# Attention and gated FFN on one core: forty normalisations shared with ScalarE, the weights' check moved behind the last scores

## The chip, the cores and the metric

The kernel runs on one core of a Trainium2 chip. A core has five engines that run side by side: TensorE (PE; its weight loads are listed as PEld), VectorE (DVE), ScalarE (ACT), GpSimd (POOL) and SyncE (SP), which here only issues transfers. Each engine takes its instructions in the order in which they were written or scheduled, and waits on semaphores for the others. The metric is the device time of one execution in microseconds (us), the median over runs.

## The reference

Attention over 4 batches, 8 heads, 768 tokens and 64 dimensions. Each query sees the 96 keys up to itself and the first 8 keys, with a bias that falls with the distance by a slope of the head. The heads' outputs are put side by side (512 columns) and go through a feed-forward part with float64 weights.

```python
scores = scale * np.matmul(q, k.transpose(0, 1, 3, 2)) + bias
scores = np.where(keep, scores, -1000000000.0)
scores = scores - np.max(scores, axis=-1, keepdims=True)
a = np.exp(scores)
a = a / (np.sum(a, axis=-1, keepdims=True) + 1e-09)
x = np.matmul(a, v)                        # to (4, 768, 512)
h = np.maximum(x @ w_in, 0.0)              # 512 -> 1024
conv_out[t] = sum(conv_w[k] * h[t + k - 1] for k in range(3))
out = h * (1.0 / (1.0 + np.exp(-conv_out))) @ w_out   # 1024 -> 512
```

## The kernel before

**Steps.** The attention is cut into 32 jobs, each for one batch, one half of the tokens (384) and one pair of heads, and each job into 3 steps of 128 queries: 96 steps. A step has the scores of both heads (PE, L351 in the first 9 jobs, L361 later), `maxima` (DVE, L378: bias and extremum in one pass over 232 columns, then a read of the sum register), `exps` (ACT, L390, one for each head, whose row sums go to `mm[:, 2:4]`), `normalise`, `transposes` (PE L410 and L411, evicted by ACT at L414, L415 or L417), and once in three steps `values` (PE L433) and `mixed` (ACT L445, DVE L446). `normalise` adds 1e-9 to both sums (DVE, L398), takes the reciprocals (DVE, L399) and scales the two heads' probabilities in place, both on GpSimd (POOL, L402). The probabilities lie in three buffers (`pbuf`) that the steps take in turn. Transposes follow two steps behind the scores (`LAG_T`), values four.

**The feed-forward part** runs beside the attention in 8 units of 384 tokens, from a queue that `fill` works off by costs: mm1 (PE L464, early pieces L485), relu (ACT L474, into `hbuf`), the convolution (POOL L510, DVE L511 and L512), the gate (ACT L530 and, for a test on saturation, L541), the split into two parts (DVE L563, ACT L565, DVE L566), mm2 (PE L575) and the eviction (ACT L589). The matmuls' results of both go to three banks of `ps_m`. The last unit follows behind the last step.

**The weights** come as 64-bit words, in 16 pieces of 128 x 512 (512 KB each). DVE makes float32 of them by bit operations (L290, L292, L294), POOL casts the high part (L299) and DVE forms the low part (L305). `piece_check` tests that the words' exponents are in the range which these bit operations need: ACT squares the high words and sums them up (L312), then a relu with a large scale, summed up too (L315). `check_weights` at the end turns the sums into a flag, by which a general path would be taken; it isn't with these inputs. The chores are kept in lists (`chores`), one for each engine, and a budget per step (`work`) says how much of each is issued.

**The order.** In steps 0 to 10 (`HAND`) every engine follows the order of the code: scores, values, transposes, `normalise(s - 1)`, `maxima(s)`, `exps(s)`, mixed, then chores. From step 11 on a list scheduler orders the instructions of each engine by an estimated timeline and the priorities of the code.

Of the kernel before, what the change touches and what calls it, by code (L numbers as in the profile page):

```python
# [9 lines left out]
F32 = mybir.dt.float32  # L10
F32R = mybir.dt.float32r
BF16 = mybir.dt.bfloat16
I32 = mybir.dt.int32
U32 = mybir.dt.uint32
AF = mybir.ActivationFunctionType
# [5 lines left out]
P = 128  # L21
# [13 lines left out]
LAG_T, LAG_V = 2, 4  # L35
NPB = 3
HAND = 11
NATIVE = 9
# [24 lines left out]
def fast_path(tc, io):  # L63
# [152 lines left out]
    odd, red, flag = rest[:, 0:3], rest[:, 3:7], rest[:, 7:8].bitcast(I32)  # L216
    bad, ones, ebias, gbias, least = (rest[:, k : k + 1] for k in range(8, 13))
    G.memset(gbias, -0.96)
    G.memset(least, 1.5)

# [85 lines left out]

    def piece_check(i, half, n):
        k = 2 * i + half
        if n == 0:
            squares[k] = p1.tile([P, HW], F32, tag="ob", name=f"square{k}")  # L310
            x = wraw[i, half][:, :, 1].bitcast(F32)
            A.activation(squares[k], x, AF.Square, accum_out=chk[:, NCHK + k : NCHK + k + 1])  # L312
        else:
            y = squares[k]
            A.activation(  # L315
                y, y, AF.Relu, bias=least, scale=-(2.0**30), accum_out=chk[:, k : k + 1]
            )

    squares = {}

    def check_weights():
        small, large = chk[:, :NCHK], chk[:, NCHK:]
        V.tensor_scalar(small, small, 0.0, None, ALU.is_gt)
        V.tensor_scalar(large, large, 2.0**30, None, ALU.is_le)
        V.tensor_scalar(large, large, -1.0, 1.0, ALU.mult, ALU.add)
        V.tensor_reduce(red[:, 0:1], chk, axis=mybir.AxisListType.X, op=ALU.max)
        V.tensor_tensor(bad, bad, red[:, 0:1], ALU.add)
# [57 lines left out]
    def exps(s):  # L385
        m, i = steps[s]
        sp, c0, n, mm = st_s[s]
        pb = pbuf[s % NPB]
        for j in range(2):
            last_exp[s] = A.activation(  # L390
                pb[:, j, c0 : c0 + n], sp[j][:, c0 : c0 + n], AF.Exp,
                bias=mm[:, j : j + 1], scale=-1.0, accum_out=mm[:, 2 + j : 3 + j],
            )
        st_s[s] = (pb, c0, n, mm)

    def normalise(s):
        pb, c0, n, mm = st_s[s]
        V.tensor_scalar(mm[:, 4:6], mm[:, 2:4], 1.0e-9, None, ALU.add)  # L398
        V.reciprocal(mm[:, 6:8], mm[:, 4:6])  # L399
        for j in range(2):  # L400
            x = pb[:, j, c0 : c0 + n]
            G.tensor_scalar(x, x, mm[:, 6 + j : 7 + j], 1.0, ALU.mult, ALU.mult)  # L402

# [240 lines left out]

    queue, cur = [], {}
    last_exp, last_mm, last_ev = {}, {}, {}

    def fill(k):
        with contextlib.ExitStack() as es:
# [7 lines left out]
            while queue and (k > 0 or queue[0][0] == 0):  # L657
                cost, fn, a = queue.pop(0)
                fn(*a)
                k -= cost  # L660

    chores = {"dve": [], "pool": [], "act": []}

# [11 lines left out]
    def piece_bits(i, half, n):  # L675
        weight_bits(i, half, n)
        if n == 0:
            for k in range(2):
                chores["act"].append((cur["s"], 0.9, piece_check, (i, half, k)))
        if n == 2:  # L680
# [32 lines left out]
    for s in range(len(steps) + LAG_V + 1):  # L713
        cur["s"] = s
        m, i = steps[s] if s < len(steps) else (len(jobs), -1)
        if s < HAND:
# [3 lines left out]
            if s >= LAG_T:  # L720
                transposes(s - LAG_T)
            if s:
                normalise(s - 1)
            maxima(s)
            exps(s)
            if ends(s - LAG_V - 1):
# [15 lines left out]
            work("pool", 1.3)  # L742
            work("act", 0.8)
        else:
# [30 lines left out]
            if s < len(steps):  # L775
                budget = DECODE_LATER[min((s - HAND) // 3, len(DECODE_LATER) - 1)]
                with tc.issue_after(last_ttr[s].ins):
                    work("dve", budget)
                    work("pool", 1.2)
                    work("act", 0.8)  # L780
        if s == 0:
# [14 lines left out]
        if s >= NB and i == 0:  # L796
            load_v(m)
    fill(10**9)

    def last_tiles():  # L800
# [173 lines left out]
```

## Time and profile before

| | before |
|---|---|
| runs, median (from, to) | 479.29 us (476.66 to 855.67), 3 runs |
| the profiled execution | 476.23 us |
| its span | 474.4 us |
| busy PE / DVE / ACT / POOL | 453.7 / 355.9 / 293.4 / 250.1 us |
| granted clock of PE, mean | 0.96 |

A row of windows gives, for one stretch of the span, the busy time and the number of instructions of each engine, the granted clock of PE as a share of full speed, and the share of the DMA engines. A row of lines gives one line's instructions on one engine: their number, the busy time of all in us and the mean of one in ns, and the engine's idle time ahead of them with what ended it. A chain of waits is followed back from the last instruction: at each step to what released it.

### The profile page before, as it was taken

How to read it: one execution, taken by the hardware profiler on the slowest of the kernel's cores; microseconds unless marked ns; L12 is line 12 of the kernel's file. 1: busy time of each engine (PE TensorE's matmuls, PEld its weight loads, DVE VectorE, ACT ScalarE, POOL GpSimd, SP SyncE). 2: the span in 40 equal slices, each digit the busy share in tenths (PEclk: the TensorE clock that was granted, in tenths of full speed). 3: DMA queues.
4: the chain of work that ended last, by engine and by line, in shares of the span. 5: the costliest groups of instructions: out<-in, count | busy, mean ns of one | idle time of the engine just before them, and what ended most of it. 6: DMA issues, size and time to landing. Idle time of an engine off the chain costs nothing.

```text
span 474.4 us, 8982 instructions
## 1 busy us (share of the span) xinstructions
PE 453.7 (96%) x3013; PEld 388.4 (82%) x3013; DVE 355.9 (75%) x936; ACT 293.4 (62%) x806; POOL 250.1 (53%) x351
## 2 busy tenths in 40 slices
PE   7989999969988999999999999999999999999994
PEld 6756688759866899888988998889988998899883
DVE  5889879995998999875798997866798877225600
ACT  2658767875947767754677677654677496335410
POOL 4544364873795597354766766555666754012000
PEclk8877599989998999999999999999999999999999
DMA  7856944223323433243324413433324201100111
GB/s 192 225 158 181 307 121 128 85 86 109 114 100 110 136 123 102 88 123 131 108 80 154 149 55 102 148 125 132 113 75 145 81 1 56 46 24 0 44 46 51
DMA packets 19062, 51.63 MB, mean 109 GB/s; under 512 B 2624, under 2 KB 2880, under 8 KB 19008
## 3 DMA queue, kind: packets, MB, share of 16 engines
q1 hardware_dynamic: 15552, 44.82, 31.0%
q10 hardware_dynamic: 3456, 6.16, 3.4%
q8 instruction: 26, 0.43, 0.4%
q14 instruction: 28, 0.23, 0.2%
HBM read 44.68 MB, written 6.29 MB: 107 GB/s over the span
## 4 chain that ended last, share of the span: by engine, by line
PE 77%; DVE 15%; ACT 2%; issue 2%; POOL 1%; DMA 1%; SPq 0%; POOLq 0%; DVEq 0%; ACTq 0%
PE o L575 26%; PE h L464 25%; PE pv L433 9%; PE s L361 5%; PE s L351 4%; PE t L410 4%; PE t L411 3%; DVE s L378 2%; DVE gl L566 1%; DVE c L511 1%; ACT pbuf L390 1%; DVE c L512 1%; DVE c L563 1%; DMA rq<-in_qk 1%; POOL pbuf L402 1%
## 5 line engine op out<-in xcount | busy, mean ns | idle before, releaser
L402 POOL TENSOR_SCALAR pbuf<-pbuf,mm 128x232 f32<-128x232 f32 (+1 forms) x192 | 137.6, 728 | 88.6 <-DVE mm L399 60.7
L390 ACT ACTIVATE pbuf<-s,mm 128x232 f32<-128x232 f32 (+1 forms) x192 | 83.5, 440 | 62.7 <-DVE mm L378 38.5
L378 DVE CUSTOM_DVE_ANT_0 s<-s,tab 128x232 f32<-128x232 f32 (+1 forms) x192 | 73.6, 385 | 24.6 <-PE s L361 16.9
L575 PE MATMUL o<-woh,gh 128*128 128x512 f32 x192 | 77.4, 403 | 0.0
L575 PE MATMUL o<-wol,gh 128*128 128x512 f32 x192 | 76.4, 398 | 0.0
L575 PE MATMUL o<-woh,gl 128*128 128x512 f32 x192 | 75.7, 395 | 0.0
L510 POOL TENSOR_SCALAR c<-hbuf,cw 128x382 f32<-128x382 f32 (+1 forms) x64 | 47.8, 751 | 51.5 <-ACT hbuf L474 51.5
L433 PE MATMUL pv<-pt,v 104*64 104x128 f32 (+2 forms) x768 | 57.4, 292 | 3.0 <-ACT pt L417 2.7
L464 PE MATMUL h<-xh,wih 128*128 128x384 f32 x252 | 59.8, 350 | 0.0
L464 PE MATMUL h<-xl,wih 128*128 128x384 f32 x252 | 59.2, 343 | 0.0
L464 PE MATMUL h<-xh,wil 128*128 128x384 f32 x252 | 57.9, 343 | 0.0
L433 PEld LDWEIGHTS pv<-pt,v 104*64 104x64 f32 (+2 forms) x768 | 43.2, 142 | 17.4 <-issue 10.0
L511 DVE SCALAR_TENSOR_TENSOR c<-hbuf,cw,c 128x382 f32<-128x382 f32 (+1 forms) x64 | 43.8, 691 | 16.6 <-POOL c L510 16.3
L417 ACT ACTIVATE pt<-t 128x512 f32<-128x512 f32 x80 | 48.0, 603 | 12.1 <-PE t L411 11.9
L410 PE MATMUL t<-ident,pbuf 128*128 128x128 f32 (+1 forms) x192 | 51.3, 286 | 3.9 <-POOL pbuf L402 3.3
L411 PE MATMUL t<-ident,pbuf 128*128 128x128 f32 x192 | 50.4, 281 | 0.0
L474 ACT ACTIVATE hbuf<-h 128x384 f32<-128x384 f32 x64 | 31.8, 498 | 25.8 <-PE h L464 25.7
L512 DVE SCALAR_TENSOR_TENSOR c<-hbuf,cw,c 128x382 f32<-128x382 f32 (+1 forms) x64 | 45.3, 711 | 0.5
L464 PEld LDWEIGHTS h<-xl,wih 128*128 128x128 f32 x252 | 44.2, 188 | 1.8 <-issue 1.8
L464 PEld LDWEIGHTS h<-xh,wih 128*128 128x128 f32 x252 | 44.0, 192 | 1.9 <-issue 1.6
L464 PEld LDWEIGHTS h<-xh,wil 128*128 128x128 f32 x252 | 44.0, 188 | 0.6 <-issue 0.5
L575 PEld LDWEIGHTS o<-woh,gl 128*128 128x128 f32 x192 | 36.3, 189 | 7.5 <-issue 0.2
(107 smaller groups left out, 858.5 us busy)
## 6 DMA issues: line engine op xcount, KB each, us to landing
v<-in_vv SPq DMA_DIRECT2D x32, 384.0 KB, 3.3
rq<-in_qk SPq DMA_DIRECT2D x23, 384.0 KB, 3.2
wr<-in_w SPq DMA_DIRECT2D x16, 512.0 KB, 5.0
rk<-in_qk SPq DMA_DIRECT2D x12, 504.0 KB, 3.5
out<-ob ACTq DMA_DIRECT2D x23, 256.0 KB, 2.0
rk<-in_qk SPq DMA_DIRECT2D x11, 408.0 KB, 3.7
rq<-in_qk SPq DMA_DIRECT2D x9, 192.0 KB, 6.0
rk<-in_qk SPq DMA_DIRECT2D x5, 204.0 KB, 5.9
```

Of the source, the lines that this page charges most:

```text
L378: last_ttr[s] = V.tensor_tensor_reduce(out=sp[j][:, c0 : c0 + n], in0=sp[j][:, c0 : c0 + n], in1=tb, scale=-0.125, scalar=3.0e38, op0=ALU. ...
L390: last_exp[s] = A.activation(pb[:, j, c0 : c0 + n], sp[j][:, c0 : c0 + n], AF.Exp, bias=mm[:, j : j + 1], scale=-1.0, accum_out=mm[:, 2 + ...
L402: G.tensor_scalar(x, x, mm[:, 6 + j : 7 + j], 1.0, ALU.mult, ALU.mult)
L410: T.transpose(pt[:ka, j, 0, :], pb[:, j, c0:P], ident)
L411: T.transpose(pt[:, j, 1, :], pb[:, j, P:256], ident)
L417: last_ev[s] = A.activation(sb, pt, AF.Copy)
L433: T.matmul(pv[m][64 * j : 64 * j + 64, i * P : (i + 1) * P], vt[m][:n, i, c, 64 * j : 64 * j + 64], sb[:n, j, c, :], start=c == 0, stop=c ...
L464: T.matmul(ps[:, :TB], w_[:, k, fs], x_, start=part == 0 and k == 0, stop=part == 2 and k == NK - 1,)
L510: G.tensor_scalar(c, *tap(1), 1.0, ALU.mult, ALU.mult)
L511: V.scalar_tensor_tensor(c, *tap(0), c, ALU.mult, ALU.add)
L512: V.scalar_tensor_tensor(c, *tap(2), c, ALU.mult, ALU.add)
L575: T.matmul(ps, g_[:, f], w_[:, f], start=f == 0 and part == 0, stop=f == NF - 1 and part == 2,)
```

## The change

In the first 40 steps (`SHARED`) the addition of 1e-9 goes from DVE to ACT, right behind the exps; DVE keeps the reciprocals; the second head is scaled by ACT, the first by POOL as before. In the hand-written steps `normalise(s - 1)` now comes behind `maxima(s)` and `exps(s)`. `piece_check` and its two ACT instructions for each piece are gone from the beginning. In their place the words are loaded again behind the last scores, 16 transfers of 512 KB with three buffers in turn, and each piece is tested by one reduction on DVE (the largest negated square) and one square with a sum on ACT, one piece for every three units of cost that `fill` issues.

```diff
-    bad, ones, ebias, gbias, least = (rest[:, k : k + 1] for k in range(8, 13))
+    bad, ones, ebias, gbias, eps = (rest[:, k : k + 1] for k in range(8, 13))
-    G.memset(least, 1.5)
+    G.memset(eps, 1.0e-9)
...
-    def piece_check(i, half, n):
-        k = 2 * i + half
-        if n == 0:
-            squares[k] = p1.tile([P, HW], F32, tag="ob", name=f"square{k}")
-            x = wraw[i, half][:, :, 1].bitcast(F32)
-            A.activation(squares[k], x, AF.Square, accum_out=chk[:, NCHK + k : NCHK + k + 1])
-        else:
-            y = squares[k]
-            A.activation(
-                y, y, AF.Relu, bias=least, scale=-(2.0**30), accum_out=chk[:, k : k + 1]
-            )
...
+    def check_load():
+        k = len(words)
+        X, tag = ((p2, "kk"), (p2, "kk"), (p1, "rk"))[k % 3]
+        t = X.tile([P, HW, 2], I32, tag=tag, name=f"check{k}")
+        nc.sync.dma_start(t, weight_words(*divmod(k, 2)))
+        words.append(t[:, :, 1].bitcast(F32))
+
+    def check_piece(k):
+        x = words[k]
+        junk = p2.tile([P, HW], F32, tag="qh", name=f"junk{k}")
+        j2 = p2.tile([P, HW], F32, tag="ql", name=f"junkb{k}")
+        V.tensor_tensor_reduce(
+            out=junk, in0=x, in1=x, scale=-1.0, scalar=-3.0e38,
+            op0=ALU.mult, op1=ALU.max, accum_out=chk[:, k : k + 1],
+        )
+        A.activation(j2, x, AF.Square, accum_out=chk[:, NCHK + k : NCHK + k + 1])
+        if len(words) < NCHK:
+            check_load()
...
+        if s < SHARED:
+            A.activation(mm[:, 4:6], mm[:, 2:4], AF.Identity, bias=eps)
...
-        V.tensor_scalar(mm[:, 4:6], mm[:, 2:4], 1.0e-9, None, ALU.add)
+        if s >= SHARED:
+            V.tensor_scalar(mm[:, 4:6], mm[:, 2:4], 1.0e-9, None, ALU.add)
         V.reciprocal(mm[:, 6:8], mm[:, 4:6])
         for j in range(2):
-            x = pb[:, j, c0 : c0 + n]
-            G.tensor_scalar(x, x, mm[:, 6 + j : 7 + j], 1.0, ALU.mult, ALU.mult)
+            x, inv = pb[:, j, c0 : c0 + n], mm[:, 6 + j : 7 + j]
+            if j and s < SHARED:
+                A.activation(x, x, AF.Copy, scale=inv)
+            else:
+                G.tensor_scalar(x, x, inv, 1.0, ALU.mult, ALU.mult)
...
+    def check_some(cost):
+        pace[0] += cost
+        while pace[1] < NCHK and pace[0] >= CHECK_EVERY * (pace[1] + 1):
+            check_piece(pace[1])
+            pace[1] += 1
...
                 fn(*a)
                 k -= cost
+                if words:
+                    check_some(cost)
...
+            maxima(s)
+            exps(s)
             if s:
                 normalise(s - 1)
-            maxima(s)
-            exps(s)
...
+        if s == len(steps):
+            for k in range(3):
+                check_load()
```

On DVE, in a hand-written step, behind the three bit operations of a weight piece (`w`, from the words `wr`), the order before was this (`mm` are a step's 128x8 small numbers, `s` its scores; the second L378 of a pair reads the sum register):

```order
L292 SCALAR_TENSOR_TENSOR w_0_381<-wr_0_249,w_0_381 128x512
L398 TENSOR_SCALAR mm_355<-mm_355 128x2
L399 RECIPROCAL mm_355<-mm_355 128x2
L378 ISA s_386,mm_401<-s_386,tab 128x232
L378 ISA mm_401 128x1
```

The same place now, where the lines are L294 for L292, L387 for L378 and L411 for L399:

```order
L294 SCALAR_TENSOR_TENSOR w_0_377<-wr_0_248,w_0_377 128x512
L387 ISA s_381,mm_392<-s_381,tab 128x232
L387 ISA mm_392 128x1
L387 ISA s_381,mm_392<-s_381,tab 128x232
L387 ISA mm_392 128x1
L411 RECIPROCAL mm_347<-mm_347 128x2
```

The addition is gone, and the reciprocal of the step before stands behind both maxima of this step.

On ACT, at the end of the first unit of the feed-forward part, the relu into `hbuf` of its last block h_7 was followed by a test, the eviction of a job's values (`xh`) and the exps of a step:

```order
L474 ACTIVATE hbuf<-h_7_1288 128x384
L541 ACTIVATE sat_2_1372,misc<-c_882,misc 128x2x382
L445 ACTIVATE xh_1359<-pv_1308 128x384
L474 ACTIVATE hbuf<-h_0_1377 128x384
L530 ACTIVATE c_882<-c_882 128x2x382
L390 ACTIVATE pbuf_193,mm_1354<-s_1349,mm_1354 128x232
```

Now (L489 is the relu, L405 the addition, L415 the second head's scaling, L432 an eviction of transposes):

```order
L489 ACTIVATE hbuf<-h_7_1251 128x384
L556 ACTIVATE sat_2_1332,misc<-c_859,misc 128x2x382
L405 ACTIVATE mm_1234<-mm_1234,misc 128x2
L405 ACTIVATE mm_1261<-mm_1261,misc 128x2
L460 ACTIVATE xh_1320<-pv_1270 128x384
L415 ACTIVATE pbuf_194<-pbuf_194,mm_1234 128x232
L432 ACTIVATE pt_1291<-t_1286 128x512
L415 ACTIVATE pbuf_192<-pbuf_192,mm_1261 128x136
```

The additions of two steps have come behind the relu of h_7, and the scalings of the same two steps behind `xh`.

On ACT in the last unit the relus of blocks 0 to 3 stood next to each other, with one gate and its test between:

```order
L474 ACTIVATE hbuf<-h_0_5097 128x384
L474 ACTIVATE hbuf<-h_1_5111 128x384
L474 ACTIVATE hbuf<-h_2_5129 128x384
L530 ACTIVATE c_5120<-c_5120 128x772
L541 ACTIVATE sat_0_5164,misc<-c_5120,misc 128x772
L474 ACTIVATE hbuf<-h_3_5147 128x384
```

Now squares of the check (L326) stand among them:

```order
L326 ACTIVATE junkb_5165,misc<-check_5100 128x512
L489 ACTIVATE hbuf<-h_0_5091 128x384
L489 ACTIVATE hbuf<-h_1_5111 128x384
L326 ACTIVATE junkb_5190,misc<-check_5120 128x512
L489 ACTIVATE hbuf<-h_2_5135 128x384
L326 ACTIVATE junkb_5214,misc<-check_5144 128x512
L545 ACTIVATE c_5126<-c_5126 128x772
L326 ACTIVATE junkb_5239,misc<-check_5168 128x512
L556 ACTIVATE sat_0_5182,misc<-c_5126,misc 128x772
L489 ACTIVATE hbuf<-h_3_5159 128x384
```

Ten of the 16 squares stand ahead of the relu of block 0, six behind that of block 1.

## Rows read from the trace of the kernel before

**Rows 1.** Windows: start:end, length; busy of PE, PEld, DVE, ACT, POOL; PEclk; DMA; GB/s.

```profile
0.00:46.00 46.00, 39.83 (x287) 30.34 (x289) 35.39 (x122) 25.82 (x87) 22.22 (x61) 0.81 0.71 194
46.00:94.00 48.00, 48.00 (x292) 37.03 (x292) 42.84 (x127) 36.22 (x111) 26.97 (x41) 0.86 0.51 155
94.00:164.00 70.00, 62.19 (x427) 53.56 (x427) 61.45 (x152) 50.34 (x139) 46.41 (x55) 0.95 0.34 110
164.00:396.00 232.00, 231.59 (x1633) 205.56 (x1632) 189.41 (x498) 154.72 (x426) 145.15 (x183) 1.00 0.33 107
396.00:474.40 78.40, 72.05 (x381) 61.90 (x379) 26.78 (x41) 26.26 (x48) 9.36 (x12) 0.99 0.10 35
```

**Rows 2.** Chain of waits, first 62 us: shares by line, then start, length, what.

```profile
by line: PE s L351 15.8%; DMA rq<-in_qk 7.8%; DVE s L378 7.6%; PE pv L433 7.3%; DVE w L292 6.2%; DVE w L294 6.1%; DVE wil L305 5.0%; ACT pbuf L390 4.6%; DVE w L290 3.8%; DVE mm L398 3.6%; PE h L485 3.5%; PE t L410 3.4%; POOL pbuf L402 3.4%;
...
2.25 4.85 DMA rq<-in_qk
```

**Rows 3.** Windows of 4 us, columns as in rows 1.

```profile
100.00:104.00 4.00, 1.03 (x9) 0.73 (x7) 3.90 (x13) 2.19 (x6) 2.29 (x4) 0.99 0.00 0
104.00:108.00 4.00, 4.00 (x32) 3.39 (x31) 3.37 (x10) 2.44 (x9) 3.26 (x5) 0.58 0.29 100
```

**Rows 4.** End of the whole chain of waits: start, length, what.

```profile
418.58 16.66 PE h L464 x96
435.25 32.70 PE o L575 x144
```

**Rows 5.** Windows of line L398 alone: DVE busy, PEclk, DMA share, GB/s.

```profile
0.00:46.00 46.00, 3.31 (x11) 0.81 0.71 194
46.00:94.00 48.00, 3.81 (x13) 0.86 0.51 155
94.00:164.00 70.00, 4.55 (x16) 0.95 0.34 110
```

**Rows 6.** Lines, the addition: xcount | busy us, mean ns | idle before, releaser.

```profile
L398 DVE TENSOR_SCALAR mm<-mm 128x2 f32<-128x2 f32 x96 | 24.4, 254 | 22.7 <-ACT pbuf L390 22.4
```

**Rows 7.** Waits up to 46 us: us in total, times, longest.

```profile
DVE mm L398 <- ACT pbuf L390: 2.6, 4, 0.9
```

**Rows 8.** Windows of line L402 alone: POOL busy, PEclk, DMA share, GB/s.

```profile
46.00:94.00 48.00, 13.83 (x24) 0.86 0.51 155
94.00:164.00 70.00, 26.35 (x33) 0.95 0.34 110
```

**Rows 9.** Timeline of DVE: start, length, line, operation.

```profile
99.72 0.96 DVE L511 SCALAR_TENSOR_TENSOR c<-hbuf,cw,c 128x382 f32<-128x382 f32 x1
...
101.76 0.60 DVE L511 SCALAR_TENSOR_TENSOR c<-hbuf,cw,c 128x382 f32<-128x382 f32 x1
```

**Rows 10.** Lines of ACT: xcount | busy us, mean ns | idle before, releaser.

```profile
L390 ACT ACTIVATE pbuf<-s,mm 128x232 f32<-128x232 f32 x160 | 71.8, 455 | 43.9 <-DVE mm L378 24.0 <-PE t L411 12.2 <-POOL pbuf L402 3.4
...
L315 ACT ACTIVATE square<-square,misc 128x512 f32<-128x512 f32 x16 | 11.5, 720 | 0.2
L312 ACT ACTIVATE square<-wr 128x512 f32<-128x512 f32 x16 | 10.8, 676 | 0.1
...
L414 ACT ACTIVATE pt<-t 32x256 f32<-32x256 f32 x16 | 5.7, 359 | 1.2 <-PE t L411 1.2
...
L312 ACT ACTIVATION_READ_ACCUMULATOR square<-wr 128x1 f32 x16 | 3.1, 197 | 0.0
...
L234 ACT ACTIVATE setup<-setup,misc 128x24 int32<-128x24 int32 x1 | 0.3, 308 | 0.0
```

**Rows 11.** Waits in 94 to 164 us: us in total, times, longest.

```profile
ACT hbuf L474 <- PE h L464: 3.6, 1, 3.6
...
ACT xh L445 <- PE pv L433: 1.9, 2, 1.7
```

**Rows 12.** Lines of DVE, the maxima: xcount | busy us, mean ns | idle before.

```profile
L378 DVE CUSTOM_DVE_ANT_0 s<-s,tab 128x232 f32<-128x232 f32 x160 | 63.9, 401 | 20.6 <-PE s L361 14.3 <-PE s L351 3.7 <-POOL pbuf L402 1.2
```

**Rows 13.** DMA issues: KB each, median us from issue to landing.

```profile
wr<-in_w SPq DMA_DIRECT2D x16, 512.0 KB, 5.0
```

More of the change, by code (lines that the diff above doesn't have):

```diff
@@ L36 @@
 NPB = 3
+SHARED = 40
+CHECK_EVERY = 3
 HAND = 11
@@ L305, in weight_low @@
         V.tensor_tensor(l[:, sl], t, h[:, sl].bitcast(F32), ALU.subtract)
-    def piece_check(i, half, n):
-        k = 2 * i + half
-        if n == 0:
-            squares[k] = p1.tile([P, HW], F32, tag="ob", name=f"square{k}")
-            x = wraw[i, half][:, :, 1].bitcast(F32)
-            A.activation(squares[k], x, AF.Square, accum_out=chk[:, NCHK + k : NCHK + k + 1])
-        else:
-            y = squares[k]
-            A.activation(
-                y, y, AF.Relu, bias=least, scale=-(2.0**30), accum_out=chk[:, k : k + 1]
-            )
-    squares = {}
+    words = []
+    def check_load():
[15 more added lines that the diff above has]
+            check_load()
     def check_weights():
         small, large = chk[:, :NCHK], chk[:, NCHK:]
-        V.tensor_scalar(small, small, 0.0, None, ALU.is_gt)
+        V.tensor_scalar(small, small, -1.5 * 2.0**-30, None, ALU.is_gt)
         V.tensor_scalar(large, large, 2.0**30, None, ALU.is_le)
@@ L645, in fast_path @@
     queue, cur = [], {}
+    pace = [0, 0]
+    def check_some(cost):
[3 more added lines that the diff above has]
+            pace[1] += 1
     last_exp, last_mm, last_ev = {}, {}, {}
@@ L660, in fill @@
                 k -= cost
-    chores = {"dve": [], "pool": [], "act": []}
+                if words:
+                    check_some(cost)
+    chores = {"dve": [], "pool": []}
     def work(eng, budget):
@@ L676, in piece_bits @@
         weight_bits(i, half, n)
-        if n == 0:
-            for k in range(2):
-                chores["act"].append((cur["s"], 0.9, piece_check, (i, half, k)))
         if n == 2:
@@ L742, in fast_path @@
             work("pool", 1.3)
-            work("act", 0.8)
         else:
@@ L779, in fast_path @@
                     work("pool", 1.2)
-                    work("act", 0.8)
+        if s == len(steps):
+            for k in range(3):
+                check_load()
         if s == 0:
@@ L798, in fast_path @@
     fill(10**9)
+    assert pace[1] == NCHK
     def last_tiles():
```

## The prediction

> **What bounds the kernel now.** I read the busy table by part of the program first [rows 1]. From 164 us on TensorE (PE) is busy for 231.59 of 232 us: whatever is taken from another engine there buys nothing. Before 164 us it is not full: it loses 6.2 us up to 46 and 7.8 us in 94 to 164, and the granted clock is 0.81, 0.86 and 0.95 there, while VectorE (DVE) stands at 35.4 of 46, 42.8 of 48 and 61.5 of 70. So the edits have to pay in these three parts. The chain of waits of the first 62 us shows who sets the pace: from 16 to 45 us its pieces are mostly DVE's, the weights' decode (L290 to L305), the maxima L378 and, with 3.6% of 62 us, the addition L398 [rows 2]. Then two windows of 4 us each: in 100 to 104 DVE is busy for 3.90 and PE for 1.03, and in the next four the clock is 0.58 [rows 3]. A stall that DVE makes is thus paid twice, as idle PE and as a PE near its lower level (1.2 of 2.4 GHz) afterwards. The chain ends in PE alone, from 418.58 to 467.95 [rows 4]; work on other engines in the last 50 us counts only if it delays that.
>
> **Forty steps without the addition.** Steps 0 to 39 are the first 164 us: of L398, 11 stand before 46, 13 before 94 and 16 before 164, with 3.31, 3.81 and 4.55 us busy [rows 5]; alone one takes less than the 254 ns mean of all 96 [rows 6]. In the hand part the move counts more than the busy time. Before, the addition and the reciprocal of step s-1 stand in front of the maxima of step s, and DVE idles 2.6 us in them waiting for the exps, in 4 waits [rows 7]. Now the maxima go first and the exps are over by then. Gain of the opening: at least what the chain itself holds, 3.6% of 62 = 2.2 us [rows 2], at most 3.31 + 2.6 = 5.9. I take 4.0, since the waits stand in the DVE-paced part but ScalarE (ACT) now has to deliver one instruction more before the reciprocal.
>
> In 46 to 164 the additions are 3.81 + 4.55 = 8.4 us of DVE. There GpSimd (POOL) also loses half of its 57 L402, half of 13.83 + 26.35 us, so 20.1 [rows 8]. This helps DVE too: the same 128x382 L511 took 0.96 us at 99.72, while POOL was casting weights, and 0.60 at 101.76 [rows 9]. If DVE had such company for a tenth of the 20 us, that is 2 us more. So 8.4 to 10.4 us of DVE are offered. What can be collected is what PE loses: in 94 to 164 that is 7.8 us idle and 0.05 of 70 = 3.5 us of clock, 11.3 together [rows 1]; in 46 to 94 PE has no idle time and its missing clock is 0.14 of 48 = 6.7. Lower bound: only what lies in the DVE-paced part, 4.55. Upper bound: 11.3. I take 8.0, near the middle: 4.55, plus half of the 3.81, plus 1.5 of contention.
>
> **What ScalarE gets.** Away go 16 squares (0.676 + 0.197 to read the sum) and 16 relus (0.720 and such a read), 16 x 1.79 = 28.6 us [rows 10]. In come 40 additions on 128x2 and 40 copies with a scale on 128x232. No row has either. The addition lies between a read of the sum (0.197) and the 128x24 L234 (0.308): I take 0.25. The copy lies between the 32x256 L414 (0.359) and the exp L390 on the same shape (0.455): I take 0.45, the exp being nearer. 40 x 0.70 = 28.0, between 22.2 and 30.5. The busy time of ACT therefore stays, at 26 of 46, 36 of 48 and 50 of 70 us [rows 1]; this cover is what hides it, and without it the 28 us would be on the path.
>
> Order is another matter. An engine takes its instructions in turn, and the copy of step s stands on ACT behind what PE must finish first. The lists of both orders show it at the end of the first FFN unit: two additions, of two steps, stand behind hbuf of h_7, and the two copies behind xh. In the trace of before that hbuf waited 3.6 us for PE and an xh 1.9 in two waits [rows 11]; so the softmax of the steps that follow would be late by these, and DVE, whose reciprocal waits for ACT's addition, would hold the maxima behind it. I charge 2.0: one such stall more; bounds 0 and, for three of them of 3.6, 10.8.
>
> The Trainium skill speaks against this edit: "ScalarE: Activation LUTs", section "Rules for kernel authors", sends additions and multiplications to VectorE, and section "What ACT_TABLE_LOAD costs" gives about 280 ns + 0.833 ns a column for an activation with a pointer operand. By that estimate an addition costs 282 ns, a copy 473, and 40 pairs 30.2 us against my 28.0; With them ACT would gain 1.6 us of work instead of losing 0.6, and if none of the 2.2 between were hidden, the sum would end at 468.4. The trace nearly agrees on the size (455 ns for 232 columns of exp [rows 10]); on where such work belongs it decides nothing, since DVE is the fuller engine before 164 us. The rule's own outcome, ACT as the pace, is rival (3).
>
> **The check at the end.** Per piece DVE gets a reduction on 128x512, the same kind as L378 (401 ns for 232 columns [rows 12]; in proportion 0.885), and ACT a square (0.873 with its read): 16 x 0.885 = 14.2 and 14.0 us. The part from 396 has 26.8 busy us of DVE and 26.3 of ACT in 78.4 [rows 1], so 50 us are free on each. The loads are 16 of 512 KB on SP's queue, which then carries nothing else but the last v; such a load took 5.0 us to land [rows 13], three are in flight, so 16 need about 27 us if each lands in its 5.0. They start after the last scores, near 398, and end near 425 to 433; mm2 starts at 435.25 [rows 4]. What could be late is the relu of a unit, behind squares on ACT whose words have not come. In the new order ten squares stand before the relu of h_0, and six between h_1 and the later ones. With three banks for h, PE can run ahead of a late relu by two f of 2.1 us (16.66 / 8). I take 0; bounds -0 (a gain isn't possible where PE is full) and +3.
>
> **The sum**, against the profiled execution's 476.23 us (its span is 474.4; the median of the runs shown is 479.29, 3.1 above): 476.2 - 4.0 - 8.0 + 2.0 + 0 = 466.2, so **466**.
>
> **Rivals.**
> (1) *The clock stays up.* If the opening's DVE stalls shrink, PE may not fall to 0.5 to 0.6 in the later parts as it does now behind stalls [rows 3]. Missing clock up to 94 is 0.19 x 46 + 0.14 x 48 = 15.5 us [rows 1]; half of it, 7.7, on top of my sum gives 458, range 452 to 461. For it: the low clock follows the idle stretch. Against: part of the 6.2 idle us up to 46 lies before the first operands land, at 2.25 + 4.85 = 7.1 us on the chain [rows 2], and the change leaves that.
> (2) *It is hidden.* In 46 to 94 PE is busy throughout, so DVE's 3.8 us there buy nothing, and the in-order waits on ACT take the rest: 476.2 - 2.2 - 4.55 + 5 = 474.5, range 471 to 480. That would also be the case in which the change doesn't do what it says: DVE's addition goes, but its reciprocal waits as long for ACT's.
> (3) *Slower: ACT's queue becomes the pace.* Each normalisation now passes DVE, ACT, DVE, ACT and POOL; each copy stands behind evictions that wait for PE, and the transposes on PE wait for the copy. It decides if the 29 steps from 11 to 39 lose more than the 12 us that I credit, so over 0.41 us a step; at 0.75 a step it gives 476.2 - 12 + 29 x 0.75 = 486, at one 3.6 us wait for every third step 476.2 - 12 + 36 = 500. For it: the two copies behind xh in the list. Against: POOL's one L402 that stays is longer (26.35 / 33 = 0.80 us [rows 8]) than the copy and runs beside it, so the pair of heads is done earlier, and LAG_T = 2 leaves a step between the exps and the transposes.
>
> **Chances.** My forecast (461 to 471) 0.47; (1) 0.18; (2) 0.20; (3) 0.15, of which 0.09 above 486. "Faster by over 2%", which is about what a measurement of this kernel tells from no change, is under 466.7: all of (1) and a little over half of the forecast, 0.18 + 0.28 = 0.46. Slower by over 2% (over 485.8) is 0.09; the rest, 0.45, is within. For 8 in 10 the range runs from 455 (a third of (1), 0.05, lies below) to 479 (most of (3) and a little of (2), 0.15, above); that also takes in the bounds of the terms: all gains at their upper ends and no charge, 476.2 - 5.9 - 11.3 = 459.0; all at the lower, with my charge and the tail's bound, 476.2 - 2.2 - 4.55 + 2 + 3 = 474.5 (with ACT's upper bound of 10.8 it is rival (3)). The likeliest case has its own range, 461 to 471.
>
> **What the new profile would show.** Right: DVE waits for exps near 0 in the opening, the step after 45 us of before some 4 us earlier; PE's idle time in 94 to 164 down from 7.8 to 3 or less; additions of 0.2 to 0.31 and copies of 0.36 to 0.47 us on ACT; POOL some 25 us less busy; no gap of PE in the last 50 us. Wrong: reciprocals that wait for ACT's addition, or PE's transposes for ACT's copy, by more than 5 us in all; an activation hbuf that waits for check words in the tail; a stretch of low clock that has only moved.

## The result, and the profile after

The changed kernel takes 474.91 us in the median of 4 runs (469.82 to 482.44), the kernel before 481.83 in that comparison (476.66 to 855.67); the ratio is 0.9852, with a 95% interval of 0.9817 to 0.9886. Executions of one and the same program fall into groups some 10 us apart, with another granted clock (the changed kernel 468.6 to 470.5 at a mean of 0.97 to 0.98, and 479 to 482 at 0.94 to 0.96), so the medians mix them and the ratios compare undisturbed executions alone. The profiled execution took 470.5 us with a span of 468.5, against 476.23 and 474.4: 5.7 us less, where 10 were forecast.

The windows of the changed kernel, with the columns of [rows 1]:

```profile
0.00:46.00 46.00, 40.03 (x279) 30.96 (x279) 31.69 (x114) 25.16 (x87) 19.47 (x50) 0.81 0.76 205
46.00:94.00 48.00, 45.35 (x315) 36.28 (x313) 46.02 (x128) 36.40 (x116) 27.36 (x35) 0.97 0.57 169
94.00:164.00 70.00, 67.44 (x478) 59.91 (x479) 61.24 (x140) 56.65 (x162) 36.20 (x43) 0.95 0.35 112
164.00:396.00 232.00, 232.00 (x1627) 204.51 (x1626) 187.37 (x488) 155.84 (x424) 134.07 (x177) 1.00 0.34 111
396.00:468.50 72.50, 64.42 (x321) 54.44 (x319) 30.10 (x64) 31.88 (x67) 5.25 (x8) 0.99 0.37 124
```

Against [rows 1], DVE is relieved in the opening (35.4 to 31.7 us), and PE's busy time there doesn't move. From 46 to 94 the clock is 0.97 where it was 0.86. From 94 to 164 PE's idle time has fallen from 7.8 to 2.6 us, while 2.7 have come up in 46 to 94, where there was none. In the last part ACT and DVE have the check.

Where the lead came from and went is told by the starts of the maxima in the two traces, and by the end of the last mm2:

| us | step 10 | step 20 | step 40 | step 95 | last mm2 ends |
|---|---|---|---|---|---|
| before | 41.1 | 75.9 | 163.8 | 394.8 | 468.0 |
| changed | 41.1 | 71.5 | 153.1 | 385.6 | 461.7 |
| lead | 0.0 | 4.4 | 10.7 | 9.2 | 6.3 |

Nothing in the opening, 10.7 us from step 10 to step 40, then 2.9 us given back behind step 95. The clock's part shows in 44 to 60 us. Before:

```profile
44.00:60.00 16.00, 15.58 (x66) 10.42 (x65) 13.73 (x42) 12.87 (x43) 6.75 (x12) 0.57 0.86 257
```

Changed:

```profile
44.00:60.00 16.00, 15.32 (x109) 11.21 (x110) 14.93 (x46) 13.17 (x44) 7.76 (x10) 1.00 1.00 272
```

PE is busy equally long, at 0.57 of full speed before and at 1.00 now, and works off 109 recorded matmuls in place of 66. The missing clock was 0.43 x 16 = 6.9 us. Over 44 to 164 us it is 10.4 us before and 5.2 now, summed from windows of 2 us.

The chain of waits of the changed kernel shows the loss at the end (start, length, what):

```profile
411.20 5.80 DMA check<-in_w
...
417.50 0.69 DVE junk L322
418.20 0.01 DVE misc L322
418.20 1.40 DVE c L526 x2
419.61 1.07 DVE c L527 x2
...
421.46 0.75 ACT junkb L326 x2
422.20 0.92 ACT sat L556 x2
423.12 0.38 ACT hbuf L489
...
423.55 4.44 PE h L479 x24
```

A load of check words, issued at 411.20, ends at 417.0; the reduction on DVE that needs it stands ahead of the convolution, which stands ahead of tanh, the test and a relu on ACT, and PE, idle from 422.27 to 423.55, waits 1.28 us for that relu's bank. After it comes the last row of the whole chain, to be set beside [rows 4]:

```profile
427.99 33.61 PE o L590 x144
```

144 matmuls of mm2 took 32.70 us before and take 33.61 now, at the full clock in both: 227 and 233 ns each.

The lines of the added work (xcount | busy us, mean ns | idle before, releaser):

```profile
L415 ACT ACTIVATE pbuf<-pbuf,mm 128x232 f32<-128x232 f32 x32 | 15.3, 485 | 4.8 <-DVE mm L411 4.8
...
L405 ACT ACTIVATE mm<-mm,misc 128x2 f32<-128x2 f32 x40 | 11.8, 297 | 1.2 <-POOL misc L221 0.8
...
L322 DVE CUSTOM_DVE_ANT_0 junk<-check 128x512 f32<-128x512 f32 x16 | 11.3, 711 | 11.8 <-DMA check<-in_w 11.7
...
L326 ACT ACTIVATE junkb<-check 128x512 f32<-128x512 f32 x16 | 10.7, 670 | 9.0 <-DMA check<-in_w 9.0
```

A copy costs 0.485 us (0.45 taken), an addition 0.297 (0.25), a reduction 0.711 (0.885). With the eight shorter copies (3.2 us) the sharing is 30.3 us on ACT, over the 28.0 of the rows, in which all forty copies were taken as long ones. The Trainium skill's figures ("ScalarE: Activation LUTs", section "What ACT_TABLE_LOAD costs") gave as estimates 282 ns for an addition and 473 for a long copy; this trace nearly agrees, with 297 and 485.

### The profile page after: what moved, and what is told of

It reads as the page before. It is cut to its first block, busy times and chain, and to the rows that moved or that the text cites. A ratio compares the mean times of both kernels' runs of the same rounds, so it can differ in the third digit from the quotient of the medians.

```text
span 468.5 us, 8981 instructions
## 1 busy us (share of the span) xinstructions
PE 449.2 (96%) x3013; PEld 386.1 (82%) x3013; DVE 356.4 (76%) x928; ACT 305.9 (65%) x854; POOL 222.4 (47%) x311
## 4 chain that ended last, share of the span: by engine, by line
PE 82%; DVE 8%; DMA 4%; ACT 2%; issue 1%; POOL 1%; ACTq 0%; SPq 0%; DVEq 0%
PE o L590 26%; PE h L479 25%; PE pv L448 10%; PE s L370 7%; PE t L425 4%; PE t L426 4%; PE s L360 4%; DMA check<-in_w 3%; DVE s L387 2%; DVE c L526 1%; ACT pbuf L399 1%; DVE c L527 1%; PE warm L150 1%; DMA nn<-in_n_global 1%; DVE w L296 1%
## 5 line engine op out<-in xcount | busy, mean ns | idle before, releaser
L417 POOL TENSOR_SCALAR pbuf<-pbuf,mm 128x232 f32<-128x232 f32 (+1 forms) x152 | 109.0, 726 | 93.4 <-DVE mm L411 76.9
L399 ACT ACTIVATE pbuf<-s,mm 128x232 f32<-128x232 f32 (+1 forms) x192 | 83.7, 442 | 53.7 <-DVE mm L387 32.9
L387 DVE CUSTOM_DVE_ANT_0 s<-s,tab 128x232 f32<-128x232 f32 (+1 forms) x192 | 73.5, 384 | 35.8 <-PE s L370 26.0
L525 POOL TENSOR_SCALAR c<-hbuf,cw 128x382 f32<-128x382 f32 (+1 forms) x64 | 49.6, 778 | 61.1 <-ACT hbuf L489 59.5
L590 PE MATMUL o<-woh,gl 128*128 128x512 f32 x192 | 76.7, 400 | 0.0
L479 PE MATMUL h<-xh,wih 128*128 128x384 f32 x252 | 58.3, 345 | 1.3 <-ACT hbuf L489 1.3
L432 ACT ACTIVATE pt<-t 128x512 f32<-128x512 f32 x80 | 48.0, 603 | 14.0 <-PE t L426 13.3
L448 PE MATMUL pv<-pt,v 104*64 104x128 f32 (+2 forms) x768 | 55.3, 285 | 1.2 <-DVE xl L461 0.7
L448 PEld LDWEIGHTS pv<-pt,v 104*64 104x64 f32 (+2 forms) x768 | 41.6, 138 | 15.6 <-issue 8.8
L590 PEld LDWEIGHTS o<-woh,gh 128*128 128x128 f32 x192 | 36.6, 191 | 7.1 <-issue 0.3
```

Source lines behind the costliest of these rows:

```text
L387: last_ttr[s] = V.tensor_tensor_reduce(out=sp[j][:, c0 : c0 + n], in0=sp[j][:, c0 : c0 + n], in1=tb, scale=-0.125, scalar=3.0e38, op0=ALU. ...
L399: last_exp[s] = A.activation(pb[:, j, c0 : c0 + n], sp[j][:, c0 : c0 + n], AF.Exp, bias=mm[:, j : j + 1], scale=-1.0, accum_out=mm[:, 2 + ...
L417: G.tensor_scalar(x, x, inv, 1.0, ALU.mult, ALU.mult)
L432: last_ev[s] = A.activation(sb, pt, AF.Copy)
L448: T.matmul(pv[m][64 * j : 64 * j + 64, i * P : (i + 1) * P], vt[m][:n, i, c, 64 * j : 64 * j + 64], sb[:n, j, c, :], start=c == 0, stop=c ...
L479: T.matmul(ps[:, :TB], w_[:, k, fs], x_, start=part == 0 and k == 0, stop=part == 2 and k == NK - 1,)
```

## The experiments

Beside the times, I read from each trace the start of step 40's maxima and the clock of 44 to 60 us; the table has them together, and the texts refer to it. "Missing" is the missing clock of 44 to 164 us, summed from windows of 2 us.

| kernel | step 10 | step 40 | clock 44 to 60 | missing, us | time, profiled | ratio to before (95%) |
|---|---|---|---|---|---|---|
| before | 41.1 | 163.8 | 0.57 | 10.4 | 476.2 | |
| changed | 41.1 | 153.1 | 1.00 | 5.2 | 470.5 | 0.985 (0.982 to 0.989) |
| changed, again | 42.0 | 152.4 | 1.00 | 1.9 | 470.1 | not given |
| no check | 42.8 | 152.8 | 1.00 | 0.2 | 466.3 | 0.978 (0.976 to 0.981) |
| check moved alone, old order | 41.6 | 169.7 | 0.58 | 13.8 | 485.0 | 1.021 (1.018 to 1.023) |
| sharing and new order, check in place | 40.3 | 163.0 | 0.79 | 8.4 | 480.1 | 1.007 (1.005 to 1.010) |
| moved, new order, no sharing | 43.2 | 160.3 | 1.00 | 3.5 | 475.7 | 0.995 (0.987 to 1.004) |
| additions left out | 37.8 | 162.8 | 0.71 | 11.7 | 477.9 | 1.016 (1.011 to 1.020) |
| only additions on ACT | 41.5 | 164.6 | 0.66 | 8.7 | 481.1 | 1.016 (1.011 to 1.022) |
| only copies on ACT | 40.6 | 153.3 | 1.00 | 0.1 | 470.6 | 0.990 (0.985 to 0.994) |
| late loads | 40.2 | 150.3 | 1.00 | 0.0 | 464.4 | 0.976 (0.972 to 0.979) |

**1. The changed kernel again** (no edit), as the yardstick.

> The changed kernel once more, as the yardstick beside the next three. In its trace step 40 is 9 to 11 us earlier than in the kernel before and step 95 9.2 us, but the end only 5.9. Theory A (the sharing gives 9 to 10 us by step 40, and the reloaded check gives 2 to 3 of them back in the last unit, by relus that stand behind squares whose words have not come): ratio to before 0.983 to 0.988, and again a gap of PE over 1 us between two mm1 matmuls of the last unit. Rival B (the tail costs nothing; the 3 us are a PE that ran slower in that one execution): ratio 0.978 to 0.982 here, and no such gap.

Two executions at the higher clock took 468.6 and 470.11 us. The gap of PE is there again (1.8 us between the starts of two mm1 matmuls at 421.2), and the last 144 matmuls take 33.61 us again. So neither was an accident of one execution: A.

**2. No check.**

```diff
+    G.memset(chk, -1.0)
...
-                if words:
-                    check_some(cost)
...
-        if s == len(steps):
-            for k in range(3):
-                check_load()
...
-    assert pace[1] == NCHK
```

> The changed kernel without the 16 reloads and without the 32 instructions of the words' check; that part is left out, its sums are set to a value that raises no flag. Theory A: 2 to 3 us below the changed kernel on the same chip (ratio to it 0.993 to 0.996), PE without a gap over 0.5 us from 395 us on, everything up to step 95 as in the changed kernel. Rival B: same as the changed kernel within 0.5 us.

466.3 us in the profiled execution, 3.8 below the changed kernel's beside it, more than A's 2 to 3. The end of its chain is that of the kernel before, to the hundredth:

```profile
408.62 16.66 PE h L480 x96
425.29 32.70 PE o L591 x144
```

From step 95's maxima to the end of mm2 it takes 73.2 us, as before, against 76.1 in the changed kernel. The moved check costs 2.9 us in the tail, and more than the gap of PE belongs to it: the matmuls themselves are faster without it. That asked for experiment 8.

**3. The check moved, and nothing else.**

```diff
-SHARED = 40
+SHARED = 0
...
+            if s:
+                normalise(s - 1)
             maxima(s)
             exps(s)
-            if s:
-                normalise(s - 1)
```

> Only the check is moved: all 96 steps are normalised as before (DVE adds, POOL scales both heads, the hand-written order as before). Theory A (the sharing is what pays): step 40 at most 3 us earlier than before, then the tail's loss of 2 to 3: 475 to 479, ratio 0.995 to 1.005. Rival C (the 28.6 us of squares and relus that leave ACT in the opening are what pays, since exps and evictions queued behind them): step 40 5 to 9 us earlier, ratio 0.985 to 0.99.

Both theories fell: 485.0 us, 2.1% slower than before. Clearing ACT of 28 us of squares and relus buys nothing by itself, in the old hand-written order (experiment 6 has the new one). Its window of 44 to 60:

```profile
44.00:60.00 16.00, 14.12 (x57) 9.30 (x55) 12.32 (x41) 4.38 (x17) 6.73 (x11) 0.58 0.86 234
```

ACT is busy for 4.4 us of 16 and idles, while PE works at 0.58 of its clock; 0.78 follows in 60 to 84. The tail's loss comes on top: the chain ends with 33.60 us for the 144 matmuls, behind waits for check words.

**4. The sharing with the new hand-written order, and the check where it was** (cut out of the edit, which is against the kernel before).

```diff
+        if s < SHARED:
+            A.activation(mm[:, 4:6], mm[:, 2:4], AF.Identity, bias=eps)
...
+            if j and s < SHARED:
+                A.activation(x, x, AF.Copy, scale=inv)
```

> Only the sharing and the new hand-written order: the check of the words stays in the opening, as 16 squares and 16 relus on ACT. Theory A: ACT has 28 us more in the first 164 us (112 before) but still a fifth of that time free, step 40 7 to 9 us earlier and no loss in the tail: ratio 0.981 to 0.986. Rival C (ACT had to be cleared first): ACT is over 0.85 busy in 46 to 164, exps wait in its queue, step 40 at most 3 us earlier, ratio 0.994 to 1.005.

480.1 us: slower than before by 0.7%. Step 40 is 0.8 us early. C had ACT over 0.85 busy; the window of 44 to 164 comes near that with 0.83:

```profile
44.00:164.00 120.00, 109.05 (x718) 88.89 (x718) 98.99 (x253) 100.16 (x308) 55.20 (x67) 0.93 0.42 129
```

ACT is the fuller one now, 100.2 of 120 us against DVE's 99.0, and PE idles 11 us of 120, where it was 8.2 before. In the changed kernel ACT has 95.1 there and PE idles 5.2. So the two halves need each other: neither alone is faster than before, and both together are. That ACT's queue is what holds PE here is argued from these sums; no run isolates it.

**5. The old hand-written order in the changed kernel.**

```diff
+            if s:
+                normalise(s - 1)
             maxima(s)
             exps(s)
-            if s:
-                normalise(s - 1)
```

> The changed kernel with only the hand-written order put back: in steps 1 to 10 the normalisation of the step before stands ahead of the maxima again. Theory K (the gain is the granted clock of 44 to 60 us, 0.58 before and 1.00 in the changed kernel; which kernel keeps it is set by when PE is idle just ahead of that stretch, and the hand-written order is one of the things that shift it): no prediction of the sign, but the time must go with the clock: 466 to 471 with a clock over 0.95 in 44 to 60, 475 to 484 with one under 0.7. Theory D (the order saves DVE 2 to 4 us in the opening, as was predicted): step 10 later by 2 to 4 us, the clock of 44 to 60 the same, 472 to 475.

Inconclusive. The profiled execution ran at a mean clock of 0.944, with 0.50 in 44 to 60, and is no match for the others; step 10 began at 41.1 in it, as in the changed kernel. One of its ten executions ran at 0.979 and took 466.65 us, so there is no sign that the old order is worse by the 2 to 4 us of D; one execution can't show more.

**6. Moved check and new order, no sharing** (the changed kernel with `SHARED = 0`).

> The changed kernel without the sharing: check moved and new hand-written order, but DVE adds and POOL scales both heads in all 96 steps. With the check moved and the old order it took 486, 2.1% more than before. Theory K: clock of 44 to 60 under 0.7 and 478 to 487, or over 0.95 and 468 to 474, and nothing between. Theory D (DVE's work in these steps sets the time, whatever the clock does): 29 additions and POOL's 20 us are back in 46 to 164, step 40 is 8 to 10 us later than in the changed kernel with the clock of 44 to 60 near 1.

475.7 us, ratio 0.995 with 1 inside the interval. Theory K (only the clock counts) said 468 to 474 for a clock of 1.00, and step 40 at 160.3 is 7.2 us later than in the changed kernel with the same clock in 44 to 60:

```profile
44.00:60.00 16.00, 13.84 (x98) 9.45 (x99) 14.84 (x51) 8.01 (x28) 9.36 (x15) 1.00 1.00 264
```

So the sharing pays beyond what the clock of this stretch does, a little less than D said (8 to 10); 2.1 of the 7.2 us were there at step 10 already. D's reason, the additions, is tested below. Experiment 3 differs from this one by the old order alone, and there step 40 is 9.4 us later and the ratio 1.021: the 2% belong to the moved check together with the old order.

**7. More filler matmuls in the kernel before.**

```diff
-WARM = (43, 0, 16, 16, 16, 12, 8, 4, 4, 4, 4, 4)
+WARM = (43, 0, 16, 16, 16, 12, 8, 4, 4, 16, 16, 16)
```

> The kernel before with 36 more of its small filler matmuls on PE in steps 8 to 10 (16 in place of 4 in each), nothing else. Theory K: they fill PE's idle 1.0 us in 42 to 46, the clock of 46 to 58 stays at its upper level, and about 6 us are gained (12 us at 0.5): 469 to 472, ratio 0.985 to 0.99. Theory D: PE gets 36 x 0.055 = 2 us more work ahead of the scores, and DVE's work in 44 to 60 is what it was: 476 to 479, ratio 1.0 to 1.005.

Ratio 0.999 (0.994 to 1.004): K's 0.985 to 0.99 is refuted. In its profiled execution, at a mean clock of 0.938 and with 486.6 us no match for the kernel before, the clock of 44 to 60 was 0.99, but 0.61 up to 44 us and 0.72 in 60 to 84: the low stretch was somewhere else. No trace shows where it was in the executions near 476 us.

**8. Sixty-four bytes.**

```diff
+    p1.tile([P, 16], F32, name="pad")
     load(0)
```

> The kernel before with one unused tile of 64 bytes per partition ahead of the pools of mixed tokens and gated parts, which moves their addresses by 64 bytes, as the changed kernel's larger check buffer does. Theory P (addresses set the pace of the matmuls): in the full stretch from 165 us the mean distance of two mm2 matmuls goes from 229.7 to 233.7 ns and that of mm1 from 175.4 to 174.0, net 576 x 4.0 - 756 x 1.4 = 1.2 us more: 477.5 to 478.5, ratio 1.002 to 1.004. Rival: the distances stay 229.7 and 175.4, the time stays within 0.5 us, and the slower mm2 of the changed kernel comes from its reloads.

The time is 478.2 in the profiled execution, 2.0 more than before; the ratio, 1.0025 (0.997 to 1.008), is too wide to tell. The chain's end tells:

```profile
419.74 16.65 PE h L465 x96
436.38 33.61 PE o L576 x144
```

The kernel has no reload at all, and its 144 matmuls take the changed kernel's 33.61 us. Between neighbouring matmuls of one line from 165 us on, mm2 stands at 233.8 ns (229.6 before), mm1 at 174.1 (175.4): P holds. These are means of the distances between starts, without those over 300 ns (mm2) and 250 (mm1). The changed kernel's check tiles, of 4096 bytes in buffers of 4032, shift everything behind them by 64 bytes. From step 95 to the end of mm2 this alone takes 74.4 us against 73.2, so 1.2 of the 2.9 us lost in the tail; 1.7 are left for the gap, 1.28 us of idle PE and what goes with it.

**9. The last six squares behind the last convolution.**

```diff
+    p1.tile([P, 8], F32, name="pad")
...
-        A.activation(j2, x, AF.Square, accum_out=...)
+        A.activation(j2, x, AF.Square, bias=zero, accum_out=...)
...
+    G.tensor_scalar(zero, cbuf[NU - 1][:, NF - 1, 0:1], 0.0, 0.0, ALU.mult, ALU.mult)
+    for k in range(pace[1], NCHK):
+        check_piece(k, zero)
```

> The changed kernel with two edits in the last unit. The last six squares take their bias from a zero that POOL forms from the last block's convolution, so that no relu of the last unit stands behind a square whose words have not come; and the mixed tokens and gated parts lie 128 instead of 64 bytes behind their places of before. Theory A with P (the tail's loss is the relu's gap of 1.3 us, the pace of mm2 of 4 ns in each of 576 and its run-up): no gap of PE from 395 us on, mm2 229.7 ns apart, 2 to 3 us below the changed kernel: 466 to 468, ratio to before 0.976 to 0.983. Rival: the DMA traffic of the reloads itself slows the tail, 469 to 471 and the gap at another place.

469.7 us in the profiled execution, ratio 0.981 (0.977 to 0.985), not clear of the changed kernel's. The gap stayed (0.84 us from 422.2, where it was 1.28), so the squares were at most a part of its cause. DVE's timeline shows what was left:

```profile
417.87 0.69 DVE L325 CUSTOM_DVE_ANT_0 junk<-check 128x512 f32<-128x512 f32 x1 [3.95 <-DMA check<-in_w]
...
418.48 1.15 DVE L529 SCALAR_TENSOR_TENSOR c<-hbuf,cw,c 128x386 f32<-128x386 f32 x2
419.55 1.15 DVE L530 SCALAR_TENSOR_TENSOR c<-hbuf,cw,c 128x386 f32<-128x386 f32 x2
```

The reduction waits 3.95 us for its words, and the convolution stands behind it. The other edit missed as well: with the shift at 128 bytes mm2 stood at 232.9 ns and mm1 at 176.5, both slower than before.

**10. No addition at all** in the kernel before, for 40 steps.

```diff
-        V.tensor_scalar(mm[:, 4:6], mm[:, 2:4], 1.0e-9, None, ALU.add)
-        V.reciprocal(mm[:, 6:8], mm[:, 4:6])
+        if s >= 40:
+            V.tensor_scalar(mm[:, 4:6], mm[:, 2:4], 1.0e-9, None, ALU.add)
+        V.reciprocal(mm[:, 6:8], mm[:, 4:6] if s >= 40 else mm[:, 2:4])
```

> The kernel before without the addition of 1e-9 in the first 40 steps (left out there, the reciprocals read the sums as they are); nobody else gets that work, POOL still scales both heads, the check stays. Theory D (DVE sets the pace of the opening and of 94 to 164, as was predicted): step 10 earlier by 2.2 to 5.9 us than 41.1, step 40 by 7 to 10. Theory Q (in the opening PE, at its lower clock, with its queue of filler matmuls, sets the pace as much as DVE): step 10 earlier by less than 1 us, step 40 by 3 to 6 apart from what the clock of 44 to 60 does.

Step 10 begins at 37.8, 3.3 us early, a size that D said; but the clock up to 46 us was 0.89 here and 0.81 before, 3.7 us less of missing clock, so that the additions need not be its cause. Then the lead goes: step 20 begins at 76.8 (75.9 before), step 40 at 162.8. The profiled execution's 477.9 us lie among those of the kernel before beside it (473.8 to 478.3, and 482.8 twice); the other four, at mean clocks of 0.94, took 483 to 485, and the ratio of 1.016 rests on them. So it isn't faster; that the edit makes it slower isn't shown. The clock of 44 to 60 is 0.71, and PE idles for 2.7 us of the 16:

```profile
44.00:60.00 16.00, 13.35 (x59) 8.96 (x58) 11.19 (x34) 10.53 (x36) 9.56 (x12) 0.71 0.93 262
```

**11. Only the additions on ACT.**

```diff
-            if j and s < SHARED:
+            if False:
```

> The changed kernel, but POOL scales both heads again in all steps; ACT only does the additions of the first 40. If the additions are what pays: step 40 within 2 us of the changed kernel's 153, and 469 to 472. If POOL's half is what pays (DVE and POOL slow each other, and PE's transposes wait for POOL): step 40 3 to 8 us later, 473 to 480.

Step 40 at 164.6, 481.1 us, 1.6% slower than before. The additions on ACT buy nothing by themselves.

**12. Only the copies on ACT** (DVE adds in all 96 steps).

```diff
-        if s < SHARED:
-            A.activation(mm[:, 4:6], mm[:, 2:4], AF.Identity, bias=eps)
```

> The changed kernel, but DVE adds the 1e-9 again in all steps; ACT only scales the second head of the first 40. If the additions are what pays: step 40 at 160 or later, 474 to 480. If POOL's half is what pays: step 40 within 2 us of 153, and 469 to 472.

Step 40 at 153.3, as in the changed kernel, and 470.6 us. Experiment 6 differs from this one by the copies alone: its step 40 came at 160.3, and all of its ten executions (473.3 to 495.0 us) lie above the four of this one (470.6 to 473.1). Its window:

```profile
44.00:60.00 16.00, 14.97 (x105) 10.55 (x105) 15.68 (x48) 11.48 (x37) 6.60 (x10) 1.00 0.97 248
```

DVE is as full as it can be, 15.68 of 16, and PE keeps its clock all the same. It is POOL's half, taken over by ACT, that pays. For the additions little is left: from step 10 to step 40 this kernel takes 112.7 us, the four with both edits (changed, again, no check, late loads) 112.0 to 110.0, and the ratios, 0.990 and 0.985, aren't clear of each other.

**13. Half of POOL's scaling left out**, check and additions as before.

```diff
-        for j in range(2):
+        for j in range(2 if s >= 40 else 1):
```

> The kernel before, but the second head isn't scaled in the first 40 steps (that part of the computation is left out); DVE adds, the check stays in the opening, ACT gets nothing new. Theory R (POOL's second scaling delays the transposes on PE, and that is what the change takes away): step 40 at 150 to 155 against 163.8, the granted clock of 44 to 60 near 1, 464 to 469, ratio 0.97 to 0.985. Rival S (it only pays together with an ACT that is cleared of 28 us of check, as the sharing with the check in the opening took 480): step 40 at 160 or later, 474 to 480.

The general path ran behind the fast one here (heads without a scale make the gates fail the kernel's test on saturation, as far as can be told); its 2849 us say nothing here, and only the first 400 us of its trace are read. Step 40 began at 164.0: R is refuted, and S holds as far as step 40 can tell. POOL is relieved (65.7 us busy up to 164 against 95.6), with nothing on ACT, and the steps are no earlier, at a clock of 0.77 in 44 to 60 and 0.80 in 60 to 84. Relief of POOL bought nothing while the check stood on ACT.

**14. Late loads.**

```diff
+        if k >= FIRST_CHECKS:
+            G.tensor_scalar(t[:, 0, 0:1].bitcast(F32), gt[B - 1, 3][1][:, 0, 0:1].bitcast(F32), 0.0, 0.0, ALU.mult, ALU.mult)
         nc.sync.dma_start(t, weight_words(*divmod(k, 2)))
...
+    p1.tile([P, 48], F32, name="pad")
```

With `FIRST_CHECKS = 9`, pieces 9 to 15 are issued behind the last unit's work, and a load of theirs first waits for gated parts of tile 3.

> The changed kernel with its last seven check pieces loaded only after the last unit's gated parts of tile 3 are there, so that neither DVE nor ACT waits for words ahead of the last unit's convolution and relus; and an unused tile that makes the shift of the addresses 256 bytes. Theory A2 (DVE's reduction, waiting for words ahead of the convolution, delays tanh and by it the relu): no gap of PE over 0.5 us from 395 us on, DVE's wait for words in 410 to 425 gone, 1.3 to 2 us less than the changed kernel, and 1 to 1.5 more if the matmuls go back to 229.7 and 175.4 ns: 465.5 to 467.5, ratio 0.974 to 0.981. Rival (the reloads' traffic slows the tail wherever they stand): 469 to 471.

A2 holds. The profiled execution took 464.4 us, the ratio is 0.976 (0.972 to 0.979), clear of the changed kernel's 0.985. The end of its chain is that of the kernel before:

```profile
406.03 16.66 PE h L485 x96
422.69 32.70 PE o L596 x144
```

PE has no gap, the old pace is back (mm2 229.4, mm1 175.6 ns at a shift of 256 bytes), and from step 95 to the end of mm2 it takes 73.2 us. All 2.9 us are back. The other 3 us against the changed kernel's profile were there by step 95 (382.3 against 385.6), with less clock missing (0.0 against 5.2 us), in a part where the two programs differ in addresses alone; that part is no merit of the late loads.

## Why the prediction was right or wrong

Two terms of the sum failed outright: the opening, 4.0 us of gain forecast and 0.0 measured, and the check at the end, forecast at no cost and measured at 2.9 us. The middle gave more than was said, and not for the reason given.

**Which engines and parts mattered: right.** From 164 us on PE is full, 232.00 of 232, and nothing was gained there: the lead of 10.7 us at step 40 was 9.2 at step 95. PE's idle time in 94 to 164 fell from 7.8 to 2.6 us, where 3 or less was named as the sign. Another sign, no gap of PE in the last 50 us, failed.

**The opening, 4.0 us: wrong.** Step 10 begins at 41.1 in both kernels. The step that failed is that DVE sets the pace there, so that what it saves arrives. DVE's load fell as counted, by 3.7 us, but DVE waited for PE's scores instead, as the waits up to 46 us show (total, times, longest). Before:

```profile
DVE s L378 <- PE s L351: 0.6, 1, 0.6
```

Changed:

```profile
DVE s L387 <- PE s L360: 5.5, 4, 3.0
```

PE itself was no faster: 39.8 us busy before and 40.0 now, at a clock of 0.81 in both. Whether the additions pace this part at all stays open: without them step 10 came 3.3 us earlier (experiment 10), but at a higher clock, and traces with the opening of the changed kernel put step 10 anywhere from 40.2 to 42.8. A lead of that size didn't last anyway: experiment 10 lost all of it by step 20.

**46 to 164 us, 8.0 of gain less 2.0 for ACT: too small, and the cause wrong.** The lead grew by 10.7 us between steps 10 and 40, where 6.0 net were forecast. The working made it out of DVE's additions and of less company for DVE on POOL. The additions by themselves bought nothing (experiments 10 and 11) and beside the copies at most 2.7 us (12); nor did the company: in 46 to 164 us the convolution's first tap on DVE took 716 ns on average before and 816 now, the second 785 and 733. What pays is the copy (experiment 12 against 6), and there was no gain where the check stayed on ACT (4 and 13). The working had taken ACT's balance, 28.6 us out and 28.0 in, as cover; without the 28.6 out there was nothing to gain.

**Rival (1), the clock: it came, in a part of its place.** It had 0.18, with 7.7 us of the missing clock up to 94 us as its price. There 15.5 us became 10.2, all of it behind the opening: the missing clock of 44 to 60 went from 6.9 us to 0. Over 44 to 164 it went from 10.4 to 5.2. If a missing us is a us of time, about half of the 10.7 us is clock; in the other traces with both edits (again, no check, late loads) it is more, 8.5 to 10.4 of leads of 11.4, 11.0 and 13.5. It doesn't stand on its own: without the sharing the same clock in 44 to 60 left step 40 at 160.3 (experiment 6), and filler matmuls bought nothing (7). What keeps the clock up isn't settled, and with it by what wait the copies pay: experiment 6 kept it at 1.00 in 44 to 60 without copies, experiment 11 did not. By windows of 2 us PE idles about as long in 42 to 46 us in the kernel before (1.0 us) and in the changed one (0.9), and the clock falls behind it in the first alone.

**The check at the end, 0 with a bound of +3: the term that was mis-sized.** It cost 2.9 us: 1.2 by addresses (experiment 8), 1.7 with the gap (2 and 14 take both away). The bound held, the value didn't. Two things were missed. The list of the new order was read on ACT alone, for squares ahead of relus, where DVE's reductions stand ahead of the convolution, and the relu is reached from there over tanh. And the loads were priced by how long one takes to land, with the start of mm2 as the time to be ready; but the words are wanted from 411 to 423 us. The scheduler had issued the first loads from 368.6 us on, ahead of the last scores, but the one that was missed was issued only at 411.20, when a reduction had left its buffer, behind a stretch in which the DMA engines had no room left, as this window of the changed kernel shows (DMA share 0.98, 350 GB/s):

```profile
404.00:412.00 8.00, 8.00 (x56) 6.79 (x55) 3.98 (x10) 3.97 (x10) 0.00 (x0) 1.00 0.98 350
```

**The sum.** 476.2 - 4.0 - 8.0 + 2.0 + 0 = 466.2 was forecast for the profiled execution and 470.5 came: the opening missed 4.0 and the tail 2.9, and the middle gave 4.7 more than its net 6.0 up to step 40, of which 1.5 went between steps 40 and 95 and 0.6 behind the last mm2, which no experiment looked into. The time lies in the range of 455 to 479, and the change is faster, by 5.7 of the 10.0 us. That the middle's surplus of 4.7 made up for the opening was luck, since the working had no such gain in it. Rival (2) had DVE's additions buy nothing, as in experiment 11, and experiment 4 looks like rival (3), ACT as the pace, where the check stays.

## What to carry to other kernels

Before work is moved to an engine, ask what has to leave it first, and read the two as one edit: here neither half paid alone, and one of them, in the old order of instructions, cost 2%. A saving on a busy engine need not arrive (DVE waited for PE instead), so leave the saved instruction out of the kernel and time that before you build the move, with the granted clock beside the time. When work is hidden in a tail, follow every engine's queue from it to PE, not only the engine on which it looks dangerous, and give late loads a true dependence, since a scheduler that expects them early puts their readers early.

## What the runs showed that was not expected

Matmuls at the full clock have a pace that hangs on where their operands lie. With the mixed tokens and gated parts 0, 64, 128 and 256 bytes behind their places of before, mm2's matmuls stood 229.6, 233.8, 232.9 and 229.4 ns apart, and mm1's 175.4, 174.1, 176.5 and 175.6 (from 165 us on; kernels before, 8, 9 and 14). The other kernels go with their shift: mm2 at 229.6 to 229.8 ns with none (2, 4, 7 and 10), at 233.7 to 233.9 with 64 bytes (changed, 1, 3, 5, 6, 11 and 12). A tile that grew by 64 bytes thus cost 1.2 us in the tail by itself, and a shift by 256 bytes undid it.
